# The second inverse stage's result written by DMA into the groups' y tiles, without the DRAM buffer between

## The chip, the core and the metric

The kernel runs on one core of a Trainium2 chip. The core has TensorE for matmuls (PE in the profile, with its weight loads as PEld), VectorE (DVE), ScalarE (ACT) and GpSimd (POOL) for elementwise work, SyncE (SP), which here issues the DMAs, and 16 DMA engines that move data between DRAM (HBM) and on-chip memory (SBUF). Matmul results land in PSUM. Each engine runs its own instructions in order and waits for others by semaphores. The metric is the device time of one execution in microseconds, smaller being better.

## The reference

Two stages follow one another over an input of 8 batches, 3136 tokens and 256 channels: a filter in the frequency domain along the tokens, and a block of Fourier mixing, normalization and a two-layer MLP.

```python
X = np.fft.rfft(x, axis=1)
y = np.fft.irfft(X * (filt_r + 1j * filt_i), n=3136, axis=1)
mixed = np.real(np.fft.fft(np.fft.fft(y, axis=1), axis=2))
u = y + mixed
un = (u - mean(u)) / np.sqrt(var(u) + 1e-06)      # over the channels
out = u + np.maximum(un @ w_ch1, 0) @ w_ch2       # 256 -> 1024 -> 256
```

The filtered spectrum is used twice: transformed back it gives y, and, since the transform of y along the tokens is that spectrum again, a second transform over the channels gives `mixed`.

## The kernel before

The transform of length 3136 = 112 x 28 is made by matmuls in two stages each way. Forward stage one (`forward1`, tiles x and s1) works on 14 pieces of a batch and stores them to a DRAM buffer d1 (L357); stage two reads them back transposed in order (at, L378), multiplies (s2), applies the filter, transposes the result by DMA (z, L427) and keeps the folded spectrum in SBUF for the channel mix (eo). Inverse stage one (`inverse1`, i1, L463 to L465) multiplies z and stores bt to a DRAM buffer d2 (L469). Inverse stage two (`inverse2`) loads d2 in seven chunks of a batch (tile b2, printed as b, L501, two buffers), multiplies (y in PSUM, L520), copies the result to the staging tile ys on ScalarE (L528, three buffers) and stores it to the DRAM buffer dy (L505): four DMAs a chunk, six for the first.

Tokens are kept as 1568 slots of a batch; a slot holds the pair of tokens of a frequency and its negative (kind 0 and 1). The MLP goes over all 8 x 1568 slots in 49 groups of 256 slots, two tiles of 128 slots each. `fetch(g)` loads a group's y from dy (L575) into a tile y of 128 x 2 x 2 x 256 floats, of which there are four. `prepare(g)` makes the channel mix (L588), adds it to y (L598), normalizes (L655 to L678), splits into high and low halves (u16, L683) and transposes by DMA (ut, L684). `first_product` (h, L706) and `second_product` (acc, L735) are the MLP in eight steps of 128 hidden channels; behind the eighth the result is added to y (L744) and stored (out, L747).

One loop over the 49 x 8 steps sets the order: in each step a first product, a second product two steps behind, then `advance` (forward stages and inverse stage one of the next batch) and `give` (steps of inverse stage two: one that loads, two that wait, seven chunks), each up to a number that follows the step. `bring` sees to it that a group's chunks are issued before it is fetched. `after(...)` puts an instruction behind a marked one on its own engine; the first fetch sets the mark ("y", 0), behind which the x loads of batch 1 are issued (L326):

```python
with after(("y", 0), ("un", 0)) if b == 1 else nullcontext():
    if q < 7:
        nc.sync.dma_start(xs[q], a["x"][b, :, 4 * q : 4 * q + 4])
```

Behind that, a scheduler orders each engine's instructions by its own estimate of times. The raw weights, loaded in the first part, share the buffers of ys and ut (`LOAD_IN`).

Of the kernel before, what the change touches and what calls it, by code (L numbers as in the profile page):

```python
# [9 lines left out]
F32 = mybir.dt.float32  # L10
# [18 lines left out]
EXPO = 0x7F800000  # L29
LAG = 2  # L30
AHEAD = 4

# [10 lines left out]
LOADED = 300  # L43
LOAD_AT = (15, 16, 17, 18, 19, 29, 30, 27)
LOAD_AFTER = (6, 7, 8, 9, 10, None, None, None)
LOAD_IN = ("ys", "ys", "ys", "ut", "ut", "ys", "ys", "ys")
WIDEN_AT = (22, 22, 30, 54, 55, 56, 57, 57)
BOUND_AT = (65, 72)
SPLIT_AT = (65, 101)
# [10 lines left out]
def slot_freqs():  # L60
    k = np.zeros((56, 28), np.int64)
    k2 = np.arange(28)
    for U in range(56):
        j, s = divmod(U, 2)
        if U == 0:
            k[0] = np.where(k2 < 14, 112 * k2, 56 + 112 * (k2 - 14))
        else:
            k1 = 28 if U == 1 else (j if s == 0 else 56 - j)
            k[U] = k1 + 112 * k2
    return k  # L70

# [18 lines left out]
def constants():  # L90
# [5 lines left out]
    for U in range(56):  # L96
        j, s = divmod(U, 2)
        th2 = 2 * np.pi * ((n2[:, None] * k[U][None]) % N) / N
        if U == 0:
            s1[:, 0, 0] = 1  # L100
            s1[:, 0, 1] = np.where(n1 % 2, -1, 1)
            lo = n2 < 14
            s2[0, 0, :, 0, :] = np.cos(th2) * lo
            s2[0, 0, :, 1, :] = -np.sin(th2) * lo
            s2[0, 1, :, 0, :] = np.cos(th2) * ~lo
            s2[0, 1, :, 1, :] = -np.sin(th2) * ~lo
            s2[0, 0, :, 1, 0] = np.where(n2 % 2, -1, 1)
        else:
            k1 = 28 if U == 1 else (j if s == 0 else 56 - j)
            th = 2 * np.pi * ((n1 * k1) % 112) / 112  # L110
            s1[:, U, 0] = np.cos(th)
            s1[:, U, 1] = -np.sin(th)
            s2[U, 0, :, 0] = np.cos(th2)
            s2[U, 1, :, 0] = np.sin(th2)
            s2[U, 0, :, 1] = -np.sin(th2)
            s2[U, 1, :, 1] = np.cos(th2)
# [38 lines left out]
    for jp in range(2):  # L155
        for kind in range(2):
            for s in range(2):
                h = s if kind == 0 or jp == 0 else 1 - s
                for q in range(28):
                    n = tok[kind, 2 * jp + s, q]  # L160
                    assert residue(h, jp) == n % 56
                    th = 2 * np.pi * ((n // 56 * j) % 56) / 56
                    a, b = 2 * np.cos(th), -2 * np.sin(th)
                    a[0] = 1
                    b[0] = (-1) ** (n // 56)
                    i2[jp, h, 0, :, 28 * kind + q] = a * 2048 / N
                    i2[jp, h, 1, :, 28 * kind + q] = b * 2048 / N

    s2h, s2l = split16(s2)
    s2h, s2l = s2h.reshape(56, 56, 56), s2l.reshape(56, 56, 56)  # L170
# [22 lines left out]
def _program(ctx, tc, nc, a, NB):  # L193
# [75 lines left out]
    for t in y16s:  # L269
        nc.gpsimd.memset(t[:, :, :, 112:], 0.0)  # L270

    sxs, alphas, dys, esps = {}, {}, {}, {}

    mF = tp.tile([128, 12], F32, tag="mF", name="mF", bufs=1)

# [212 lines left out]
            load(c + far)  # L488

    def inverse2(b, d2):  # L490
        dy = dp.tile([2, NS, 256], F32, tag="dy", name=f"dy_{b}", bufs=3)
        dys[b] = dy
        d2v = d2.rearrange("(m r) j l c -> (r j l) m c", r=2)
        al = alphas[b]
        bts = {}

        def load(c):
            if c < 7:
                bts[c] = fp.tile([112, 4, 2, 256], F16, tag="b2", name=f"b2_{b}_{c}", bufs=2)
                with after("dy"):  # L500
                    nc.sync.dma_start(bts[c].rearrange("p j h c -> p (j h) c"), d2v[:, 8 * c : 8 * c + 8])  # L501

        def store(k, s, r, ys, c, j0):
            rows = dy[k, 224 * c : 224 * c + 224].rearrange("(j s q) c -> s q j c", j=4, s=2)
            marks["dy"] = nc.sync.dma_start(rows[s, :, j0], ys[r : r + 28, j0]).ins  # L505

        load(0)
        for _ in range(1 + WAIT):
            yield
        for c in range(7):  # L510
            load(c + 1)
            bt = bts.pop(c)
            ys = fp.tile([128, 4, 256], F32, tag="ys", name=f"ys_{b}_{c}", bufs=3)
            ps = [bank(f"y_{b}_{c}_{o}").rearrange("p (j c) -> p j c", j=2) for o in range(2)]
            with after("pe") if c == 0 else nullcontext():
                for o, p in enumerate(ps):
                    for js, t in [(slice(0, 1), 0), (slice(1, 2), 1)] if c == o == 0 else [(slice(0, 2), 1)]:
                        for i in range(2):
                            for h in range(2):
                                nc.tensor.matmul(  # L520
                                    p[64 * h : 64 * h + 64, js],
                                    i2[:, t, h, i],
                                    bt[:, 2 * o + js.start : 2 * o + js.stop, h],
                                    start=i == 0,
                                    stop=i == 1,
                                )
            for o, p in enumerate(ps):
                nc.scalar.activation(ys[:, 2 * o : 2 * o + 2], p, AF.Copy, scale=al[:, 2:3])  # L528
            for s in range(2):
                store(0, s, 64 * s, ys, c, slice(0, 4))  # L530
                if c:
                    store(1, s, 64 * (1 - s) + 28, ys, c, slice(0, 4))
                else:
                    store(1, s, 64 * s + 28, ys, c, slice(0, 1))
                    store(1, s, 64 * (1 - s) + 28, ys, c, slice(1, 4))
            yield

    d2s = {}
# [25 lines left out]

    ys_of = {}

    def fetch(g):
        y = ys_of[g] = mp.tile([128, 2, 2, 256], F32, tag="y", name=f"y_{g}", bufs=4)
        for t, (g0, g1) in enumerate(groups[g]):
            q = g0  # L570
            while q < g1:
                b = q // NS
                e = min(g1, (b + 1) * NS)
                with after(("ut", 0)) if g == 2 else after(("out", g - 4)):
                    marks["y", g] = nc.sync.dma_start(  # L575
                        y[q - g0 : e - g0, t], dys[b][:, q - b * NS : e - b * NS].rearrange("k s c -> s k c")
                    ).ins
                q = e

    def channels(p, lhs, start, stop):  # L580

# [187 lines left out]
    def load_weights(i):  # L769
        name = ("w1", "w2")[i // 4]  # L770
        src = a[name][:, i % 4 // 2, 512 * (i % 2) : 512 * (i % 2) + 512]
        if a[name].dtype == F32:
            words[i] = src
            return
        pool, bufs = {"ut": (mp, 2), "ys": (fp, 3)}[LOAD_IN[i]]
        words[i] = pool.tile([128, 512, 2], I32, tag=LOAD_IN[i], name=f"raw_{i}", bufs=bufs)
        with after(("d1", LOAD_AFTER[i])):
            nc.sync.dma_start(words[i], src.bitcast(I32).rearrange("p (n w) -> p n w", w=2))

    def widen_weights(i):  # L780
        name = ("w1", "w2")[i // 4]
        if i % 4 == 0:
            raws[name] = [], tp.tile([128, 5], F32, tag="mw", name="m" + name)
        ws, m = raws[name]
        if name == "w1":
            w = mp.tile([128, 512], F32, tag="h", name=f"w_{i}", bufs=4)
        else:
            if i % 2 == 0:
                pairs[0] = mp.tile([128, 2, 512], F32, tag="y", name=f"w_{i}", bufs=4)
            w = pairs[0][:, i % 2]  # L790
        ws.append(w)
        if a[name].dtype == F32:
            nc.sync.dma_start(w, words[i])
        else:
            with after("ylo" if "ylo" in marks else ("dve", 13)):
                widen(w, words[i], f"{i}")
        squares(m[:, i % 4 : i % 4 + 1], w, f"{i}")
# [32 lines left out]

    nc.sync.dma_start(s1, a["c_s1"])
    forth, home = steps(there), steps(back)
    done, come = [0], [0]

    def advance(n):

# [7 lines left out]
    def give(n):  # L844

        while come[0] < min(n, NB * BACK) and done[0] >= STEPS * (come[0] // BACK + 1) - 1:
            next(home)
            come[0] += 1

# [45 lines left out]
    while come[0] < need(255):  # L895
        weigh(STEPS + come[0])
        give(come[0] + 1)
    fetch(0)
# [6 lines left out]
    fetch(1)  # L905
    work = prepare(1)
    for _ in range(AHEAD):
        next(work, None)
# [1 line left out]
    for q in range(8 * ng + LAG):  # L910
        g, f = divmod(q, 8)
        if g < ng:
            first_product(g, f)
        if f == 8 - AHEAD:
            for _ in work:
                pass
            if g + 2 < ng:
                work = prepare(g + 2)
        next(work, None)
        if q >= LAG:  # L920
            second_product(*divmod(q - LAG, 8))
        advance(int(STEPS * (1 + min((q + 1) / RISE, (q + 1) / per + EARLY))))
        give(min(come[0] + 1, soon(32 * q + SOON)))
        if f == 0 and g + 2 < ng:
            bring(groups[g + 2][-1][1] - 1)
            fetch(g + 2)


def device_arrays(x, filt_r, filt_i, moe_w_ch1, moe_w_ch2):
# [51 lines left out]
```

## Time and profile before

| | us |
|---|---|
| median of 3 runs | 1581.63 |
| lowest and highest of them | 1572.67, 1591.9 |
| profiled execution, span from first to last instruction | 1585.0 |
| busy PE, DVE, ACT, POOL in it | 1407.5, 1092.9, 771.9, 541.5 |

The profile gives no time of that execution beside its span. It was taken in one execution; the span in 40 equal slices of 39.6 us, each digit the busy share or the granted clock in tenths, shows the two parts:

```profile
PE   4443899888989889899989999899999999999998
DVE  7774787677767776687756876687766876554552
PEclk9555899989999989999999999999999999999999
DMA  7989468879985787748983689748983799544321
```

In the first four slices the first batch goes through its stages, TensorE is less than half busy and its granted clock is about half; behind them the MLP runs and TensorE is busy nearly throughout, while the DMA engines have a cycle of some 180 us, one batch. A row of the waits names the engine and line that waited, what released it, the total, the number and the longest; a row of the timeline gives start and duration, and in brackets the idle time before it.

### The profile page before, as it was taken

What the parts mean: (1) busy time and instruction counts of PE and PEld (TensorE: products, weight loads), DVE (VectorE), ACT (ScalarE), POOL (GpSimd) and SP (SyncE); (2) the same over time, 40 slices, a digit from 0 to 9 for tenths busy, and PEclk for the clock granted to TensorE, in tenths of its full rate; (3) what the DMA queues carried; (4) which work ended last, traced back from release to release, by engine and by line L of the source; (5) the groups of instructions that cost most, each with busy time, mean ns of one, the idle gap of its engine ahead of it and who ended that gap; (6) DMA issues with size and microseconds to landing.
All of it is one profiled execution on the core that took longest, in us unless ns stands there. A gap on an engine that the chain in (4) does not pass through costs nothing.

```text
span 1585.0 us, 30178 instructions
## 1 busy us (share of the span) xinstructions
PE 1407.5 (89%) x11217; PEld 940.7 (59%) x11217; DVE 1092.9 (69%) x2409; ACT 771.9 (49%) x1442; POOL 541.5 (34%) x675
## 2 busy tenths in 40 slices
PE   4443899888989889899989999899999999999998
PEld 1331566545766557566766666665765667666666
DVE  7774787677767776687756876687766876554552
ACT  4455364365536445365544545365554655434432
POOL 4462019405711266004821076003830086001100
PEclk9555899989999989999999999999999999999999
DMA  7989468879985787748983689748983799544321
GB/s 226 257 204 240 109 157 182 199 196 197 200 224 129 179 172 177 193 128 203 220 221 86 192 194 194 208 126 196 210 228 97 196 216 182 133 110 124 78 67 41
DMA packets 446260, 273.13 MB, mean 172 GB/s; under 512 B 235392, under 2 KB 412592, under 8 KB 446112
## 3 DMA queue, kind: packets, MB, share of 16 engines
q1 hardware_dynamic: 446112, 271.20, 71.3%
q8 instruction: 88, 1.44, 0.4%
q14 instruction: 60, 0.49, 0.1%
HBM read 113.31 MB, written 102.76 MB: 136 GB/s over the span
## 4 chain that ended last, share of the span: by engine, by line
PE 63%; DMA 17%; DVE 10%; POOL 3%; issue 3%; ACT 3%; SPq 1%; DVEq 0%; ACTq 0%; POOLq 0%
PE h L706 25%; PE acc L735 23%; PE s L353 4%; DMA b<-d 4%; PE y L520 3%; DMA z<-y 3%; DMA d<-bt 3%; DMA ut<-u 2%; DMA at<-d 2%; PE mix L588 2%; DVE y L598 2%; DVE mx L262 2%; DVE h L716 1%; DMA d<-ast 1%; PE i L463 1%
## 5 line engine op out<-in xcount | busy, mean ns | idle before, releaser
L706 PE MATMUL h<-ut,w1s 128*128 128x512 f16 x2352 | 598.4, 389 | 20.1 <-DMA ut<-u 17.1
L735 PE MATMUL acc<-w2s,h 128*128 128x256 f16 x4704 | 599.0, 274 | 1.9 <-DVE y L744 1.9
L735 PEld LDWEIGHTS <-h 128*128 128x128 f16 x4704 | 456.9, 98 | 143.0 <-issue 17.0
L716 DVE SCALAR_TENSOR_TENSOR h<-h,h 128x512 f16<-128x512 f32 x392 | 268.1, 685 | 304.7 <-ACT h L715 303.8
L715 ACT ACTIVATE h<-h 128x512 f16<-128x512 f32 x392 | 233.2, 595 | 450.2 <-PE h L706 443.8
L706 PEld LDWEIGHTS <-w1s 128*128 128x128 f16 x2352 | 227.2, 99 | 240.2 <-issue 43.7
L683 POOL TENSOR_TENSOR u<-un,u 128x512 f16<-128x512 f32 x94 | 108.4, 1167 | 729.6 <-ACT u L681 633.7
L598 DVE SCALAR_TENSOR_TENSOR y<-mix,alpha,y 128x508 f32<-128x508 f32 (+1 forms) x368 | 156.2, 475 | 16.8 <-PE mix L588 14.7
L520 PE MATMUL y<-b,i 112*64 112x512 f16 (+1 forms) x480 | 76.5, 424 | 55.8 <-DMA b<-d 49.2
L422 POOL TENSOR_TENSOR y<-yt,y 128x448 f16<-128x448 f32 x105 | 110.9, 1058 | 33.8 <-ACT y L418 33.3
L678 ACT ACTIVATE un<-y,sb 128x256 f32<-128x256 f32 x196 | 101.7, 590 | 32.4 <-DVE sb L671 30.4
L353 PE MATMUL s<-x,s 112*112 112x512 f16 x336 | 106.8, 415 | 9.6 <-DVE x L348 5.0
L468 DVE TENSOR_TENSOR bt<-i,bt 112x512 f16<-112x512 f32 x112 | 75.8, 682 | 53.7 <-ACT bt L467 53.2
L528 ACT ACTIVATE ys<-y,alpha 128x512 f32<-128x512 f32 x112 | 75.3, 685 | 74.2 <-PE y L520 74.0
L414 POOL TENSOR_TENSOR yt<-yt,t 128x224 f32<-128x224 f32 x105 | 69.1, 658 | 116.4 <-DVE t L410 62.3
L467 ACT CAST bt<-i 112x512 f16<-112x512 f32 x112 | 65.1, 582 | 80.5 <-PE i L465 70.5
L356 DVE TENSOR_TENSOR ast<-s,ast 112x512 f16<-112x512 f32 x112 | 76.6, 684 | 29.0 <-ACT ast L355 25.9
L348 DVE SCALAR_TENSOR_TENSOR x<-x,sx,x 112x512 f16<-112x512 f32 x111 | 87.9, 802 | 6.0 <-ACT x L347 5.8
L401 PE MATMUL s<-s,at 112*128 112x56 f16 x896 | 64.0, 192 | 30.9 <-DMA at<-d 22.4
L347 ACT ACTIVATE x<-x,sx 112x512 f16<-112x512 f32 x111 | 78.9, 724 | 22.3 <-DVE sx L259 20.8
L463 PE MATMUL i<-z,i 112*112 112x256 f16 x224 | 65.7, 293 | 26.4 <-DMA z<-y 19.6
L418 ACT CAST y<-yt 128x448 f16<-128x448 f32 x112 | 62.5, 563 | 51.6 <-POOL yt L415 46.7
(129 smaller groups left out, 1611.7 us busy)
## 6 DMA issues: line engine op xcount, KB each, us to landing
x<-x SPq DMA_DIRECT2D x56, 448.0 KB
d<-ast SPq DMA_DIRECT2D x112, 224.0 KB
at<-d SPq DMA_DIRECT2D x56, 448.0 KB
d<-bt SPq DMA_DIRECT2D x112, 224.0 KB
b<-d SPq DMA_DIRECT2D x56, 448.0 KB
out<-y SPq DMA_DIRECT2D x98, 256.0 KB
y<-dy SPq DMA_DIRECT2D x92, 256.0 KB
dy<-ys SPq DMA_DIRECT2D x208, 112.0 KB
```

Source lines behind the costliest of these rows:

```text
L348: nc.vector.scalar_tensor_tensor(x16[:, 1], x, sx[:112, 1:2], x16[:, 0], op0=ALU.mult, op1=ALU.subtract)
L353: marks["pe", q] = nc.tensor.matmul(p, s1[:, hs], x16[:, hx], start=i == 0, stop=i == 2).ins
L422: last = half(b, hf == 1).tensor_tensor(y16[:, :, 1, :112], ytv, y16[:, :, 0, :112], op=ALU.subtract)
L463: nc.tensor.matmul(p[:, i], i1[:, j + i, 0], z[:, i, 0], start=True, stop=False)
L520: nc.tensor.matmul(p[64 * h : 64 * h + 64, js], i2[:, t, h, i], bt[:, 2 * o + js.start : 2 * o + js.stop, h], start=i == 0, stop=i == 1,)
L598: nc.vector.scalar_tensor_tensor(out, p, al, y, op0=ALU.mult, op1=ALU.add)
L678: nc.scalar.activation(un[:m, k], y[:m, t, k], AF.Identity, bias=sb[:m, i, 1:2], scale=sb[:m, i, 3:4])
L683: marks["u16", g] = low.tensor_tensor(u16[:m, :, :, 1], unv, u16[:m, :, :, 0], op=ALU.subtract).ins
L706: marks["pe"] = nc.tensor.matmul(p[:, c0 : c0 + n].rearrange("p (t k q) -> p t k q", k=2, q=m), w1s[:, d, hw, 128 * f : 128 * f + 128], ut ...
L715: nc.scalar.activation(h[:, 0, :nt], p[:, :nt], AF.Relu)
L716: marks["h"] = nc.vector.scalar_tensor_tensor(h[:, 1, :nt], p[:, :nt], 0.0, h[:, 0, :nt], op0=ALU.max, op1=ALU.subtract).ins
L735: nc.tensor.matmul(acc[:m, k], h[:, hh, c0 : c0 + m], w2s[:, f, hw], start=f == 0 and k == 0 and i == 0, stop=f == 7 and k == 1 and i == 2,)
```

## The change

- `dy`, `store` and `fetch` go. `place` writes rows of ys by DMA straight into the y tiles of the groups. One DMA carries 56 slots (or 28, in the first rows of a batch) of one j and one kind, and is split where a tile of 128 slots ends.
- The two residues of a pair are now j and j + 28 for both kinds (k1 = j + 56 s in place of j and 56 - j), and the columns of the i2 constants are set so that a half of ys (64 rows) holds 56 slots of one kind.
- A y tile is taken when its first slot is written (`y_tile`). There are five of them, and two of ys instead of three. The raw weights that lay in ys lie in y tiles.
- `give` does not issue a chunk, nor the three steps ahead of chunk 0, while the chunk's last slot lies in a group that needs more than five tiles beyond the groups finished (`gone`).
- The marks ("y", g), and with them the order of the loads of x of batch 1, have gone with `fetch`.

```diff
-LOAD_IN = ("ys", "ys", "ys", "ut", "ut", "ys", "ys", "ys")
+LOAD_IN = ("y", "y", "y", "ut", "ut", "y", "y", "y")
...
-            k1 = 28 if U == 1 else (j if s == 0 else 56 - j)
+            k1 = 28 if U == 1 else j + 56 * s
...
-                h = s if kind == 0 or jp == 0 else 1 - s
+                h = kind if jp else s
+                col = 28 * (s if jp else kind)
...
-        dy = dp.tile([2, NS, 256], F32, tag="dy", name=f"dy_{b}", bufs=3)
...
-        def store(k, s, r, ys, c, j0):
-            rows = dy[k, 224 * c : 224 * c + 224].rearrange("(j s q) c -> s q j c", j=4, s=2)
-            marks["dy"] = nc.sync.dma_start(rows[s, :, j0], ys[r : r + 28, j0]).ins
+        def place(ys, r, n, j, kind, slot):
+            while n:
+                tile_, p = divmod(slot, 128)
+                m = min(n, 128 - p)
+                y = y_tile(tile_ // 2)
+                marks["dy"] = nc.sync.dma_start(y[p : p + m, tile_ % 2, kind], ys[r : r + m, j]).ins
+                r, n, slot = r + m, n - m, slot + m
...
-            ys = fp.tile([128, 4, 256], F32, tag="ys", name=f"ys_{b}_{c}", bufs=3)
+            ys = fp.tile([128, 4, 256], F32, tag="ys", name=f"ys_{b}_{c}", bufs=2)
...
-            for s in range(2):
-                store(0, s, 64 * s, ys, c, slice(0, 4))
-                if c:
-                    store(1, s, 64 * (1 - s) + 28, ys, c, slice(0, 4))
-                else:
-                    store(1, s, 64 * s + 28, ys, c, slice(0, 1))
-                    store(1, s, 64 * (1 - s) + 28, ys, c, slice(1, 4))
+            for j in range(4):
+                slot = b * NS + 224 * c + 56 * j
+                for h in range(2):
+                    if c or j:
+                        place(ys, 64 * h, 56, j, h, slot)
+                    else:
+                        for kind in range(2):
+                            place(ys, 64 * h + 28 * kind, 28, j, kind, slot + 28 * h)
...
-    def fetch(g):
-        y = ys_of[g] = mp.tile([128, 2, 2, 256], F32, tag="y", name=f"y_{g}", bufs=4)
...
-                with after(("ut", 0)) if g == 2 else after(("out", g - 4)):
-                    marks["y", g] = nc.sync.dma_start(
...
+    def y_tile(g):
+        if g not in ys_of:
+            ys_of[g] = mp.tile([128, 2, 2, 256], F32, tag="y", name=f"y_{g}", bufs=YBUFS)
+        return ys_of[g]
...
+            b, c = divmod(come[0], BACK)
+            c -= 1 + WAIT
+            if (b * NS + 224 * max(c, 0) + 223) // 256 >= gone[0] + YBUFS:
+                return
             next(home)
             come[0] += 1
...
             second_product(*divmod(q - LAG, 8))
+            gone[0] = (q - LAG + 1) // 8
```

The scheduler then gives another order. At the end of inverse stage one of batch 4, on ScalarE, before (h16 is the relu behind eight such h of a group, sb, un and u16 belong to the normalization of group 22, ys_4_0 is the first copy out of the second inverse stage; the last copy of inverse stage one, bt_4_6_1, stands two rows above the first row):

```order
L715 ACTIVATE h16_21_0_10043<-h_21_0_10036 128x512
L662 ACTIVATE sb_22_10022<-mv_22_10012,eps_88 128x4
L715 ACTIVATE h16_21_1_10073<-h_21_1_10066 128x512
L678 ACTIVATE un_22_0_10076<-y_22_9721,sb_22_10022 128x256 x2
L678 ACTIVATE un_22_1_10134<-y_22_9721,sb_22_10022 128x256 x2
L715 ACTIVATE h16_21_2_10131<-h_21_2_10124 128x512
L681 CAST u16_22_0_10079<-un_22_0_10076 128x4x128
L528 ACTIVATE ys_4_0_10101<-y_4_0_0_10102,alpha_4_8472 128x512
```

And now, with the same rows above the first:

```order
L714 ACTIVATE h16_21_0_10185<-h_21_0_10178 128x512
L457 CAST eo_89<-ef_4_6_10324 128x2x160
L661 ACTIVATE sb_22_10164<-mv_22_10154,eps_88 128x4
L714 ACTIVATE h16_21_1_10212<-h_21_1_10205 128x512
L677 ACTIVATE un_22_0_10215<-y_22_9114,sb_22_10164 128x256 x2
L677 ACTIVATE un_22_1_10250<-y_22_9114,sb_22_10164 128x256 x2
L680 CAST u16_22_0_10218<-un_22_0_10215 128x4x128
L714 ACTIVATE h16_21_2_10247<-h_21_2_10240 128x512
L680 CAST u16_22_1_10253<-un_22_1_10250 128x4x128
L714 ACTIVATE h16_21_3_10278<-h_21_3_10271 128x512
L714 ACTIVATE h16_21_4_10300<-h_21_4_10293 128x512
L533 ACTIVATE ys_4_0_10354<-y_4_0_0_10355,alpha_4_8594 128x512
```

The copy to ys, and on TensorE the y matmuls that it reads, stand behind h_21_3 and h_21_4 now, two steps of the MLP later.

On SP, where batch 5 goes from forward stage one (stores of ast to d1) to stage two (loads of at), before (ys_4_3 is a chunk of batch 4):

```order
L357 DMA d1_5_10216<-ast_5_12_10808 112x1024
L357 DMA d1_5_10216<-ast_5_13_10855 112x1024
L505 DMA dy_4_9998<-ys_4_3_10955 28x4x256
L684 DMA_TRANSPOSE ut_24_10738<-u16_24_0_10828 128x8x128
L684 DMA_TRANSPOSE ut_24_10738<-u16_24_1_10872 128x8x128
L378 DMA at_5_0_10894<-d1_5_10216 112x8x256
```

And now, with the last d1 store, ast_5_13, three rows above the first row:

```order
L509 DMA y_26_10621<-ys_4_2_10993 48x256
L509 DMA y_26_10621<-ys_4_2_10993 8x256
L509 DMA y_26_10621<-ys_4_2_10993 48x256
L509 DMA y_26_10621<-ys_4_2_10993 56x256
L683 DMA_TRANSPOSE ut_24_10873<-u16_24_0_10960 128x8x128
L509 DMA y_26_10621<-ys_4_2_10993 56x256
L509 DMA y_26_10621<-ys_4_2_10993 24x256
L509 DMA y_27_11015<-ys_4_2_10993 32x256
L509 DMA y_26_10621<-ys_4_2_10993 24x256
L509 DMA y_27_11015<-ys_4_2_10993 32x256
L683 DMA_TRANSPOSE ut_24_10873<-u16_24_1_11032 128x8x128
L380 DMA at_5_0_11054<-d1_5_10332 112x8x256
```

The chunk's placements and the transposes of group 24 stand between that store and the load.

On SP again, in the first part, where the y tiles of groups 0 and 1 are loaded and the x loads of batch 1 (x_1) follow, before (the last stores of inverse stage one, bt_0_6, and the first loads b2_0 stand some ten rows above):

```order
L575 DMA y_0_1151<-dy_0_1077 128x2x256
L501 DMA b2_0_3_1172<-d2_0_115 112x8x256
L575 DMA y_0_1151<-dy_0_1077 128x2x256
L575 DMA y_1_1346<-dy_0_1077 128x2x256
L326 DMA x_1_0_1404<-x 112x1024
L326 DMA x_1_1_1405<-x 112x1024
L505 DMA dy_0_1077<-ys_0_2_1174 28x4x256 x4
L501 DMA b2_0_4_1199<-d2_0_115 112x8x256
L326 DMA x_1_2_1406<-x 112x1024
L326 DMA x_1_3_1407<-x 112x1024
```

And now, with x_1_0 to x_1_3 directly above the first row:

```order
L328 DMA x_1_4_1404<-x 112x1024
L328 DMA x_1_5_1405<-x 112x1024
L328 DMA x_1_6_1406<-x 112x1024
L471 DMA d2_0_115<-bt_0_6_0_1056 112x1024
L471 DMA d2_0_115<-bt_0_6_1_1067 112x1024
L501 DMA b2_0_0_1077<-d2_0_115 112x8x256
L501 DMA b2_0_1_1079<-d2_0_115 112x8x256
L509 DMA y_0_1098<-ys_0_0_1081 28x256 x4
L509 DMA y_0_1098<-ys_0_0_1081 56x256 x2
```

The x loads of batch 1 have moved ahead of the last stores of inverse stage one and of the first loads of stage two.

More of the change, by code (lines that the diff above doesn't have):

```diff
@@ L31 @@
 AHEAD = 4
+YBUFS = 5
 PAUSE = 4
@@ L108, in constants @@
         else:
-            k1 = 28 if U == 1 else (j if s == 0 else 56 - j)
+            k1 = 28 if U == 1 else j + 56 * s
             th = 2 * np.pi * ((n1 * k1) % 112) / 112
@@ L165, in constants @@
                     b[0] = (-1) ** (n // 56)
-                    i2[jp, h, 0, :, 28 * kind + q] = a * 2048 / N
-                    i2[jp, h, 1, :, 28 * kind + q] = b * 2048 / N
+                    i2[jp, h, 0, :, col + q] = a * 2048 / N
+                    i2[jp, h, 1, :, col + q] = b * 2048 / N
     s2h, s2l = split16(s2)
@@ L270, in _program @@
         nc.gpsimd.memset(t[:, :, :, 112:], 0.0)
-    sxs, alphas, dys, esps = {}, {}, {}, {}
+    sxs, alphas, esps = {}, {}, {}
     mF = tp.tile([128, 12], F32, tag="mF", name="mF", bufs=1)
@@ L490, in inverse2 @@
     def inverse2(b, d2):
-        dy = dp.tile([2, NS, 256], F32, tag="dy", name=f"dy_{b}", bufs=3)
-        dys[b] = dy
         d2v = d2.rearrange("(m r) j l c -> (r j l) m c", r=2)
@@ L565, in _program @@
     ys_of = {}
-    def fetch(g):
-        y = ys_of[g] = mp.tile([128, 2, 2, 256], F32, tag="y", name=f"y_{g}", bufs=4)
[L569 to L573, printed above, removed]
-                with after(("ut", 0)) if g == 2 else after(("out", g - 4)):
[L575 to L578, printed above, removed]
+    def y_tile(g):
+        if g not in ys_of:
+            ys_of[g] = mp.tile([128, 2, 2, 256], F32, tag="y", name=f"y_{g}", bufs=YBUFS)
+        return ys_of[g]
     def channels(p, lhs, start, stop):
@@ L774, in load_weights @@
             return
-        pool, bufs = {"ut": (mp, 2), "ys": (fp, 3)}[LOAD_IN[i]]
+        pool, bufs = {"ut": (mp, 2), "y": (mp, YBUFS)}[LOAD_IN[i]]
         words[i] = pool.tile([128, 512, 2], I32, tag=LOAD_IN[i], name=f"raw_{i}", bufs=bufs)
@@ L788, in widen_weights @@
             if i % 2 == 0:
-                pairs[0] = mp.tile([128, 2, 512], F32, tag="y", name=f"w_{i}", bufs=4)
+                pairs[0] = mp.tile([128, 2, 512], F32, tag="y", name=f"w_{i}", bufs=YBUFS)
             w = pairs[0][:, i % 2]
@@ L832, in _program @@
     forth, home = steps(there), steps(back)
-    done, come = [0], [0]
+    done, come, gone = [0], [0], [0]
     def advance(n):
@@ L897, in _program @@
         give(come[0] + 1)
-    fetch(0)
     for i, _ in enumerate(prepare(0)):
@@ L904, in _program @@
     bring(511)
-    fetch(1)
     work = prepare(1)
@@ L925, in _program @@
             bring(groups[g + 2][-1][1] - 1)
-            fetch(g + 2)
 def device_arrays(x, filt_r, filt_i, moe_w_ch1, moe_w_ch2):
```

## The prediction

> **What bounds the kernel now.** I read the page first (engines, chain), then TensorE's own waits, then the places of the longest ones, then SP's queue. The page says who is full and who carries the end:
>
> ```profile
> PE 1407.5 (89%) x11217; PEld 940.7 (59%) x11217; DVE 1092.9 (69%) x2409; ACT 771.9 (49%) x1442; POOL 541.5 (34%) x675
> PE 63%; DMA 17%; DVE 10%; POOL 3%; issue 3%; ACT 3%; SPq 1%; DVEq 0%; ACTq 0%; POOLq 0%
> ```
>
> TensorE bounds the steady part, and DMA waits are the next share of the chain. TensorE's waits from 165 us to the end (us in total, times, longest):
>
> ```profile
> PE y L520 <- DMA b<-d: 28.4, 7, 6.5
> PE h L706 <- DMA ut<-u: 17.1, 7, 5.8
> PE s L401 <- DMA at<-d: 12.6, 12, 2.2
> ```
>
> The largest is the one beside the change: seven times, once for each batch from 1 to 7, TensorE stands before the first matmul of the second inverse stage (y, L520) until its input b has come back from DRAM. These are the seven places in TensorE's timeline:
>
> ```profile
> 316.00 1.06 PE L520 MATMUL y<-b,i 112*64 112x256 f16 x12 [3.27 <-DMA b<-d]
> ...
> 464.69 1.92 PE L520 MATMUL y<-b,i 112*64 112x256 f16 x12 [3.74 <-DMA b<-d]
> ...
> 653.98 1.92 PE L520 MATMUL y<-b,i 112*64 112x256 f16 x12 [5.54 <-DMA b<-d]
> ...
> 830.26 1.92 PE L520 MATMUL y<-b,i 112*64 112x256 f16 x12 [6.49 <-DMA b<-d]
> ...
> 1012.14 1.92 PE L520 MATMUL y<-b,i 112*64 112x256 f16 x12 [4.12 <-DMA b<-d]
> ...
> 1190.00 1.06 PE L520 MATMUL y<-b,i 112*64 112x256 f16 x12 [3.09 <-DMA b<-d]
> ...
> 1367.74 1.06 PE L520 MATMUL y<-b,i 112*64 112x256 f16 x12 [2.16 <-DMA b<-d]
> ```
>
> Around the longest, the chain (start, us, what) shows two transfers in series and then TensorE slow, beside its usual pace:
>
> ```profile
> 807.08 1.30 PE h L706 x6
> ...
> 808.77 1.31 PE acc L735 x12
> ...
> 817.01 8.28 DMA d<-bt
> 825.36 4.86 DMA b<-d
> 830.26 1.92 PE y L520 x12
> ...
> 833.90 2.56 PE h L706 x6
> ```
>
> Six h matmuls take 1.30 us before the wait and 2.56 us after it. The granted clock (the figure after POOL's busy time) in short windows behind six of the seven waits says why:
>
> ```profile
> 316.00:318.00 2.00, 2.00 (x17) 1.08 (x17) 0.25 (x3) 1.26 (x2) 0.00 (x0) 1.00 0.24 43
> 465.00:469.00 4.00, 4.00 (x24) 2.24 (x21) 0.00 (x0) 1.37 (x2) 0.00 (x0) 0.64 0.31 69
> 654.00:658.00 4.00, 4.00 (x18) 1.81 (x18) 0.00 (x0) 1.37 (x2) 0.00 (x0) 0.50 0.60 143
> 830.00:837.00 7.00, 6.74 (x33) 3.81 (x33) 0.00 (x0) 2.39 (x4) 1.15 (x1) 0.53 0.69 177
> 1012.00:1018.00 6.00, 5.86 (x32) 3.13 (x32) 0.00 (x0) 1.76 (x3) 0.00 (x0) 0.55 0.72 197
> 1190.00:1194.00 4.00, 4.00 (x27) 2.24 (x27) 0.07 (x1) 1.86 (x3) 0.00 (x0) 0.69 0.47 133
> ```
>
> At batches 2 to 6 the loss by the lower clock is 4 x 0.36 + 4 x 0.50 + 7 x 0.47 + 6 x 0.45 + 4 x 0.31 = 10.7 us on top of the wait itself; at batch 1 nothing.
>
> **The change: the wait for b.** The diff does not touch this load, but it adds a gate (a chunk is not started before one of five y tiles is free), and the order that is built from it puts more MLP matmuls between the last matmul of the first inverse stage and the first y. Counted on TensorE in the two orders, h and acc matmuls between them are, for batches 1 to 7, before: 12+34, 24+41, 24+48, 24+36, 24+44, 18+36, 24+41; now: 18+40, 90+179, 42+84, 36+72, 30+60, 24+48, 24+37. At 1.30/6 and 1.31/12 us each, with 0 to 24 small mix matmuls (estimated at 0.06 us, about half an acc matmul), the cover was 7.3, 10.2, 10.4, 9.1, 10.0, 7.8, 10.6 us and is 9.2, 40.7, 19.2, 16.6, 14.0, 11.3, 10.2 us. Old cover plus old wait is what the two transfers need: 10.6, 13.9, 15.9, 15.6, 14.1, 10.9, 12.8 us. Need less new cover leaves 1.4, 0, 0, 0, 0.1, 0, 2.6: about 4 us of the 28.4. So 24 us of waiting and the 10.7 us of slow clock go: -35 us. Against it: a wait that goes can return at the next one. The nearest rows are the 17.1 and 12.6 us above, nineteen waits, spread over the batches; if TensorE comes some 5 us earlier to one of them per batch, up to all 35 us returns. Ends: 0 and -35. I take -32, nearer the full end, because the at wait starts from a store of TensorE's own earlier result and moves with it, and the ut covers (below) mostly grow.
>
> **SP's queue.** All DMAs are issued by SP in order. Removed are 240 stores to dy and 104 loads of y from it; added are 631 placements (12 to 14 for the first chunk of a batch, 10 to 12 for each other, split where a tile ends). Their prices, and what the loads waited for (durations min/median/max in ns; then us in total, times, longest):
>
> ```profile
> L505 SPq DMA_DIRECT2D dy<-ys x240: 307/403/2717, 123.6 to 1480.5; - x120
> ...
> L575 SPq DMA_DIRECT2D y<-dy x104: 304/390/1746, 129.1 to 1504.9; - x104
> ```
>
> ```profile
> SPq L575 <- DMA out<-y: 72.5, 31, 5.2
> ...
> SPq L575 <- DMA dy<-ys: 24.7, 24, 2.7
> ```
>
> Issue: 631 x 0.40 = 252 us against 240 x 0.403 + 104 x 0.390 = 137 us, +115 us. The loads' waits, 97 us, go: the first placement into a tile now stands behind the output store of the group five before, mostly ten rows or more behind it, and the wait for dy does not exist. Net +18 us over 49 groups on a queue that is no bound by itself; bounds -97 and +115. But a burst of a dozen placements is 5 us in which a transpose or an at load stands behind them. One place shows it: for batch 5, eleven placements and two transposes stand between the last d1 store and the first at load (before: one store and two transposes), 10 x 0.4 = 4 us more, and the cover there grows by only 1.6 us. I take +8 us for TensorE: 2.4 at this place, and 0.13 at each of the 42 other chunks after the head. Ends 0 and +42 (a whole microsecond at each).
>
> Here a rule of the Trainium skill speaks against the change: "DMA: Bandwidth & Descriptors", section Bandwidth, calls transfers under 64 KB dominated by descriptors, and the placements are 56 KB and less where the stores were 112 KB. By its fit of 2.0 us plus bytes over 436 GB/s a placement of 56 KB is an estimated 2.1 us, and a chunk's twelve, if they went one behind the other, an estimated 25 us; the sum would then come out on the side of the second rival. Row L505 shows a queue that goes on after 0.40 us, so the sum stays with the row, and whether the landings pile up no row of this trace can say.
>
> **DMA traffic.** 25.7 MB written and 25.7 MB read become 25.7 MB from SBUF to SBUF.
>
> ```profile
> q1 hardware_dynamic: 446112, 271.20, 71.3%
> ```
>
> A packet takes 0.713 x 16 x 1585 us / 446112 = 40 ns on average; 25,088 packets of 1 KB fewer are 25,088 x 40 ns / 16 = 63 us of 1130 us. That is off the path except where the DMAs are full: ends 0 and -4 (6% of the 58 us of waits above), I take -2.
>
> **The head, to the first h.** The x loads of batch 1 were ordered behind the first y load; that mark is gone, and they now stand ahead of the last two stores of the first inverse stage (third place shown with the change). The chain, the DMA share (the figure before GB/s) and the rows around the first h:
>
> ```profile
> 4.08 11.79 DMA x<-x
> ...
> 115.02 2.24 DMA d<-bt
> 117.28 4.05 DMA b<-d
> ...
> 136.62 9.68 DMA b<-d
> 146.31 7.95 DMA y<-dy
> ```
>
> ```profile
> 105.00:110.00 5.00, 1.74 (x9) 1.32 (x7) 3.74 (x8) 2.69 (x5) 1.70 (x3) 0.50 0.62 121
> 110.00:115.00 5.00, 3.15 (x13) 2.47 (x13) 4.62 (x9) 2.62 (x7) 1.34 (x1) 0.50 0.39 117
> ```
>
> ```profile
> 156.01 5.18 SPq L684 DMA_TRANSPOSE ut<-u  x2
> ```
>
> ```profile
> 164.87 4.06 PE L706 MATMUL h<-ut,w1s 128*128 128x512 f16 x12
> ...
> 191.35 2.76 PE L706 MATMUL h<-ut,w1s 128*128 128x512 f16 x12 [1.40 <-DMA ut<-u]
> ```
>
> Seven x loads took 11.8 us at the start; put in at about 110 us they run to 121.5, so the stores land near 123 instead of 117.3: +6 us. Behind that the long 9.68 and 7.95 us, stretched by these same x loads, shrink to about the 4.05 us of an undisturbed b load, and the y loads are gone. But SP now issues 56 placements before ut instead of 22 stores and 4 loads (+30 x 0.4 = 12 us), and ScalarE writes chunk 3 only behind the normalization of group 0. I put ut at about 161 (156.01 before) and h at 167: +2 us. Chunks 5 and 6 of batch 0 move behind it: 16 matmuls at half of the 1.92 us for 8 that the head pays, +2 us. Group 1 is ready earlier: -1.4 us. Together +3; ends -6 (only the y loads' 7.95 us go, less 2) and +10 (the 6 us and 4 of SP's 12 come through).
>
> **The covers of ut.** Counted the same way, TensorE's work between a group's last mix and its first h falls by 2.4, 6.0, 2.3, 1.8 and 4.0 us at groups 3, 4, 8, 12 and 37 and grows by 6 to 10 us at groups 5, 11, 17, 23 and 29. Group 4 waits already:
>
> ```profile
> 291.68 5.30 PE L706 MATMUL h<-ut,w1s 128*128 128x512 f16 x12 [1.65 <-DMA ut<-u]
> ```
>
> There 6.0 us come in full, at group 12 perhaps 1: +7 less the b wait of batch 1 that goes: I take +5; ends -5 and +14.
>
> **At nothing.** The new pairing of residues changes constants alone: matmuls, ScalarE's copies and POOL's work stay the same in number, and POOL issues no DMA. The raw weights now lie in y tiles, and the first placement needs one that VectorE's widening has read; that is done while b is loaded, and if it were not, SP would stand there.
>
> **Sum.** -32 + 8 - 2 + 3 + 5 = -18, against the profiled span of 1585.0 us (the profile gives no time beyond it): 1567. That span is 3.4 us above the median of the three runs, 1581.63; from the median it is 1563.6, and I say 1563 us.
>
> **Rivals.**
> - *The wait moves (within 1%).* For it: chain work beside the b wait (8.28 us for d<-bt) is DMA, and waits for ut and at of 29.7 us follow. Against: the covers there. If half of the 35 us returns: -18 + 14.5 = -3.5, 1578 us. The y loads' trip through DRAM was hidden in the steady part anyway: it is no wait of TensorE's above.
> - *SP becomes the bound (slower).* The placements' landing times hold SP back: 12 in a row, and ut and z transposes behind them. It decides from 18/42 = 0.43 us lost on TensorE at each of 42 chunks beyond the +8. At a whole 1.0 us each and the b gain halved: -16 + 42 - 2 + 3 + 5 = +32, 1614 us. For it: bursts of 12 against 4. Against: the 97 us of waits that SP loses. The page of the Trainium skill named above is on this side.
> - *The y tile is free too late (slower).* A placement waits for the output store five groups back and blocks SP as the loads did, 72.5 us in all now. That is paid today with four tiles, so it costs more only where placements that stand on SP keep ScalarE from its two ys tiles, and TensorE from its banks: at the longest wait, 5.2 us, once a batch, 7 x 5.2 - 18 = +18, 1600 us. Against: in the new order the store stands ten rows or more ahead at most tiles.
>
> **Chances.** Forecast (faster, 1540 to 1566) 0.52, the wait moves 0.28, SP 0.12, the tile 0.08. Within 1%, 15.8 us, is about what a measurement of this kernel cannot tell from no change. So faster 0.52, same 0.30, slower 0.18. The range runs from -41 (all of -35, the head's -6, the rest 0) to +12, short of the two slower cases: 1540 to 1594. The forecast's own is 1540 to 1566.
>
> **What would show it.** Right: the y waits on b below 6 us in all, the clock at 1.00 behind most of them, SP's waits for out smaller than 72 us, first h between 162 and 172 us. Wrong: TensorE's waits for ut or at above 45 us together; ScalarE's ys or SP's placements waiting for DMA in tens of microseconds; the first h after 175 us.

## The result, and the profile after

| | before | changed |
|---|---|---|
| median, us | 1583.04 (1572.67 to 1591.9, 4 runs) | 1651.84 (1642.66 to 1655.15, 4 runs) |
| ratio, 95% interval | | 1.0427 (1.0382 to 1.0473) |

The changed kernel is slower by 4.3%; the prediction was 1563 us. The page of the changed kernel: its span and its chain by engine and by line (the kernel before had PE 63% and SPq 1%), and its DMA queue:

```profile
span 1647.5 us, 30693 instructions
PE 1418.1 (86%) x11217; PEld 946.4 (57%) x11217; DVE 1091.0 (66%) x2409; ACT 772.2 (47%) x1442; POOL 542.6 (33%) x675
PEclk9555799789999999999999999998999999999999
q1 hardware_dynamic: 424464, 245.52, 62.1%
PE 46%; DMA 18%; POOL 9%; issue 9%; DVE 9%; SPq 5%; ACT 3%; DVEq 0%; ACTq 0%; POOLq 0%
```

The engines' work is the same (TensorE's 1418.1 us against 1407.5 go with its lower clock, 0.926 against 0.939 in the mean), and the DMA engines do less; TensorE's share of the chain fell, and time in which SP issues DMAs entered it. TensorE's longest waits from 165 us on (total, times, longest):

```profile
PE h L705 <- DMA ut<-u: 54.3, 16, 13.4
PE i L465 <- DMA z<-y: 20.4, 8, 4.6
PE y L525 <- DMA b<-d: 16.0, 7, 3.9
PE s L403 <- DMA at<-d: 13.8, 11, 3.1
```

The wait for b went from 28.4 to 16.0 us, but ut from 17.1 to 54.3, and z from the 5.5 us of this row of the kernel before to 20.4. Of the 54.3 us, 13.4 are the wait for the first h itself, which in the kernel before came at 164.87 us without a wait for ut; behind the first h it is 40.9 us against 17.1. The row of z before:

```profile
PE i L463 <- DMA z<-y: 5.5, 6, 1.8
```

Both are transposes that SP issues behind placements. The placement's own row (durations in ns, minimum, median, maximum) tells why:

```profile
L509 SPq DMA_DIRECT2D y<-ys x632: 532/746/2996, 130.5 to 1554.3; - x158
```

A placement holds SP for 746 ns at the median, not for the 403 ns of a store to dy. SP's timeline in the head (start, us, what) has them back to back, five chunks ahead of the first ut, and TensorE's first h behind that:

```profile
130.48 9.38 SPq L509 DMA_DIRECT2D y<-ys  x12
139.96 0.47 SPq L501 DMA_DIRECT2D b<-d  x1
140.54 8.63 SPq L509 DMA_DIRECT2D y<-ys  x12
...
175.59 2.65 SPq L683 DMA_TRANSPOSE ut<-u  x2
```

```profile
180.23 4.22 PE L705 MATMUL h<-ut,w1s 128*128 128x512 f16 x12 [13.35 <-DMA ut<-u]
```

The first h was at 164.87 us: 15.4 us of the span's 62.5 are lost here. The other 47.1 us are lost behind it: from the first h to the end TensorE is idle 31.0 us longer (112.8 against 81.8) and busy 16.2 us longer with much the same matmuls (1354.5 against 1338.3, at a granted clock of 0.96 against 0.97). One such place is the longest later wait, of 7.21 us. There GpSimd has written the second half of u (two instructions, the last over at 807.21), and SP comes to the second transpose 11 us later, with nine placements of 6.3 us among the rows between. The rows are GpSimd's, SP's and TensorE's:

```profile
804.94 2.27 POOL L682 TENSOR_TENSOR u<-un,u 128x512 f16<-128x512 f32 x2 [2.47 <-ACT u L680]
```

```profile
809.37 1.26 SPq L429 DMA_TRANSPOSE z<-y  x1
810.68 2.73 SPq L509 DMA_DIRECT2D y<-ys  x4
813.52 1.26 SPq L683 DMA_TRANSPOSE ut<-u  x1
814.83 3.55 SPq L509 DMA_DIRECT2D y<-ys  x5
818.50 1.25 SPq L683 DMA_TRANSPOSE ut<-u  x1
```

```profile
821.62 2.74 PE L705 MATMUL h<-ut,w1s 128*128 128x512 f16 x6 [7.21 <-DMA ut<-u]
```

### The profile page after: what moved, and what is told of

The parts are those of the page before. It is cut to its first block, busy times and chain, and to the rows that moved or that the text cites. A ratio compares the mean times of both kernels' runs of the same rounds, so it can differ in the third digit from the quotient of the medians.

```text
span 1647.5 us, 30693 instructions
## 1 busy us (share of the span) xinstructions
PE 1418.1 (86%) x11217; PEld 946.4 (57%) x11217; DVE 1091.0 (66%) x2409; ACT 772.2 (47%) x1442; POOL 542.6 (33%) x675
## 3 DMA queue, kind: packets, MB, share of 16 engines
q1 hardware_dynamic: 424464, 245.52, 62.1%
## 4 chain that ended last, share of the span: by engine, by line
PE 46%; DMA 18%; POOL 9%; issue 9%; DVE 9%; SPq 5%; ACT 3%; DVEq 0%; ACTq 0%; POOLq 0%
PE h L705 18%; PE acc L734 17%; DMA d<-bt 4%; SPq L509 4%; PE s L355 3%; DMA ut<-u 3%; DMA z<-y 3%; PE y L525 2%; DMA at<-d 2%; DVE y L597 2%; POOL y L424 2%; DMA b<-d 2%; DMA d<-ast 2%; POOL yt L417 2%; DMA x<-x 2%
## 5 line engine op out<-in xcount | busy, mean ns | idle before, releaser
L705 PE MATMUL h<-ut,w1s 128*128 128x512 f16 x2352 | 603.5, 392 | 59.5 <-DMA ut<-u 54.3
L355 PE MATMUL s<-x,s 112*112 112x512 f16 x336 | 102.3, 407 | 9.4 <-DVE x L350 5.8
L416 POOL TENSOR_TENSOR yt<-yt,t 128x224 f32<-128x224 f32 x105 | 69.1, 658 | 112.8 <-DVE t L412 52.5
L408 DVE TENSOR_TENSOR yt<-s,ft 128x448 f32<-128x448 f32 x112 | 68.3, 615 | 36.5 <-PE s L404 31.2
```

The source lines that it names most:

```text
L355: marks["pe", q] = nc.tensor.matmul(p, s1[:, hs], x16[:, hx], start=i == 0, stop=i == 2).ins
L705: marks["pe"] = nc.tensor.matmul(p[:, c0 : c0 + n].rearrange("p (t k q) -> p t k q", k=2, q=m), w1s[:, d, hw, 128 * f : 128 * f + 128], ut ...
```

## The experiments

The theory to test: the issue of a placement costs SP 0.75 us, and what stands behind a burst comes late (issue theory). Its rivals: the transfers from SBUF to SBUF are slow or crowd the DMA engines, whoever issues them (landing theory); the gate, five y tiles and two ys tiles gave a worse order (order theory); the x loads of batch 1, put ahead, are the loss. All ratios are against the kernel before, run on the same chip. Each kernel is scheduled anew from its source, so neighbours of an edit move too; single waits are compared with that in mind.

**The price by itself (`price`).** Rows of twelve DMAs (K is 12), one shape after the other, on a chip that does nothing else. The part that issues them within SBUF:

```diff
+    def rows(n, w=256, p=0, r=0):
+        def issue(q, dst, src):
+            for i in range(K):
+                q.dma_start(dst[p : p + n, i, :w], src[r : r + n, i, :w])
+        return issue
```

> No part of the computation: rows of twelve DMAs back to back, one shape after the other, first all issued by SP, then all by ScalarE, with nothing else under way. Issue theory: from SBUF to SBUF, 56 rows of 1 KB hold SP for 0.70 to 0.80 us, 16 and 32 rows for 0.55 to 0.60; 28 rows to DRAM 0.30 to 0.40. The price goes with the number of rows and the destination, not with the bytes of a row. Landing or contention theory: with nothing else under way each placement holds SP for 0.45 us or less, as a store to DRAM does, and the 0.75 us of the changed kernel comes from full queues.

Issue durations from SP, by time: SBUF to SBUF with rows of 1 KB, 16, 28, 32, 56 and 128 rows, and 56 rows of 512 bytes; then to DRAM with 28 and 112 rows; then 56 rows, SBUF to SBUF, issued by ScalarE:

```profile
L214 SPq DMA_DIRECT2D dst<-src x12: 560/587/588, 18.8 to 25.7; - x12
...
L214 SPq DMA_DIRECT2D dst<-src x12: 746/746/762, 41.8 to 50.5; - x12
...
L214 SPq DMA_DIRECT2D dst<-src x12: 555/589/594, 54.4 to 61.3; - x12
...
L214 SPq DMA_DIRECT2D dst<-src x12: 746/746/799, 88.4 to 97.1; - x12
...
L214 SPq DMA_DIRECT2D dst<-src x12: 508/599/601, 134.9 to 141.9; - x12
...
L214 SPq DMA_DIRECT2D dst<-src x12: 746/746/829, 145.8 to 154.7; - x12
...
L221 SPq DMA_DIRECT2D buf<-src x12: 369/383/384, 209.8 to 214.5; - x12
...
L221 SPq DMA_DIRECT2D buf<-src x12: 308/444/452, 248.4 to 253.6; - x12
...
L214 ACTq DMA_DIRECT2D dst<-src x12: 757/763/794, 371.9 to 380.8; - x12
```

746 ns for 56 rows without any other traffic: the price is the instruction's own, not contention. In the shapes tried it depends on the destination and on the number of rows; for 56 rows it is the same with rows of 1 KB and of 512 bytes.

**The order alone (`before_gate`).** The kernel before with the gate, five y tiles, two ys tiles and the raw weights in y tiles; results still go through dy.

```diff
+            if (b * NS + 224 * max(c, 0) + 223) // 256 >= gone[0] + YBUFS:
+                return
...
-            ys = fp.tile([128, 4, 256], F32, tag="ys", name=f"ys_{b}_{c}", bufs=3)
+            ys = fp.tile([128, 4, 256], F32, tag="ys", name=f"ys_{b}_{c}", bufs=2)
```

> The kernel before (results still through DRAM), with only the order part of the change: five y tiles, two ys tiles, the raw weights in y tiles, and the gate in give. Issue theory: SP issues what it did, 1570 to 1595 us, TensorE's waits for ut below 25 us. Order theory: the 47 us that the changed kernel loses behind the first h come from here, 1615 to 1640 us.

1575.06 us, ratio 0.9977 (0.9955 to 0.9998); first h at 161.62 us. The order costs nothing, so the order theory falls. The issue theory had its number for ut wrong too: the waits for ut are above its 25 us. TensorE's waits from 165 us on, all behind the first h:

```profile
PE h L707 <- DMA ut<-u: 31.0, 13, 5.3
PE s L402 <- DMA at<-d: 14.2, 9, 5.8
PE i L464 <- DMA z<-y: 11.3, 6, 3.9
PE y L521 <- DMA b<-d: 6.4, 3, 4.1
```

The wait for b does shrink from 28.4 to 6.4 us here, as predicted, but ut, at and z together take back 13.9, 1.6 and 5.8 us.

**More issues in the kernel before (`before_split`, `split_half`).** The stores to dy cut into four, with the same bytes: in the first all of them, in the second those of one kind.

```diff
-            marks["dy"] = nc.sync.dma_start(rows[s, :, j0], ys[r : r + 28, j0]).ins
+            for j in range(j0.start, j0.stop):
+                marks["dy"] = nc.sync.dma_start(rows[s, :, j], ys[r : r + 28, j]).ins
```

> The kernel before, but each store to DRAM is split into its four parts: 896 stores of 28 rows of 1 KB instead of 240 of 28 rows of 4 KB, the same bytes. At 0.43 us from one to the next SP gets some 280 us more to issue (the changed kernel has 632 x 0.75 - 137 = 337 us more than the kernel before). Issue theory: 1610 to 1640 us, first h at 172 us or later, TensorE's waits for ut above 40 us. Order or landing theory: 1575 to 1595 us.

> The kernel before, with the stores of one kind split into four as in the run with all of them split: 560 stores instead of 240, some 138 us more on SP (896 stores and some 280 us made +74 us). If every microsecond of SP costs alike: about +36 us, 1605 to 1625 us. If the first 100 us or so are free and the loss sets in behind them (half the placements on GpSimd left SP with about 100 us more than the kernel before, at no loss): (138 - 100) / (280 - 100) x 74 = about +16 us, 1588 to 1602 us. GpSimd has no part in it.

`before_split`: 1653.66 us, ratio 1.0466 (1.0421 to 1.0512), more than the issue theory's 1640. `split_half`: 1585.69 us, ratio 1.0040 (1.0019 to 1.0061), less than both of its ranges. Rows of the first: the stores, TensorE's first h, and its waits from 165 us on (11.6 us of ut and 5.9 of b lie at or ahead of the first h):

```profile
L506 SPq DMA_DIRECT2D dy<-ys x896: 306/383/2441, 123.4 to 1551.6; - x180
```

```profile
183.40 4.33 PE L707 MATMUL h<-ut,w1s 128*128 128x512 f16 x12 [11.64 <-DMA ut<-u]
```

```profile
PE h L707 <- DMA ut<-u: 41.4, 16, 11.6
PE y L521 <- DMA b<-d: 35.9, 8, 7.8
PE i L463 <- DMA z<-y: 25.6, 11, 8.7
```

The whole loss appears without one transfer from SBUF to SBUF and without the new order: the landing theory falls as the main cause. And it is not proportional: 320 added stores cost 6 us, 656 cost 74.

**The destination of the pieces (`to_dram`).** The changed kernel; pieces that don't end a tile go to DRAM, and other data fills the y tile, so y is not the reference's.

```diff
+                to = y[p : p + m, tile_ % 2, kind] if p + m == 128 else dy[p : p + m, tile_ % 2, kind]
+                marks["dy"] = nc.sync.dma_start(to, ys[r : r + m, j]).ins
```

> The changed kernel, with its 632 pieces, but those that do not reach the end of a tile of 128 slots go to a DRAM buffer, and a y tile is filled by one load of other data (so y is not the reference's). 436 issues fall from about 0.7 us to 0.43, 49 loads of 0.4 come in: some 100 us less on SP, and more DRAM traffic. Issue theory: the loss goes down by a third or so, 1620 to 1638 us, first h at 174 us or earlier. Order theory: 1643 us or more.

1612.18 us, ratio 1.0211 (1.0172 to 1.0251), first h at 172.87 us: half of the loss goes, more than expected, with the same number of pieces and more DRAM traffic.

**Another queue (`half_act`, `half_pool`, `quarter_pool`, `all_pool`).** The same placements, some or all issued by another engine. The edit of `half_pool`; `half_act` has nc.scalar in it, `quarter_pool` the condition j == 3, and `all_pool` nc.gpsimd for all:

```diff
-                marks["dy"] = nc.sync.dma_start(y[p : p + m, tile_ % 2, kind], ys[r : r + m, j]).ins
+                q = nc.gpsimd if r >= 64 else nc.sync
+                marks["dy"] = q.dma_start(y[p : p + m, tile_ % 2, kind], ys[r : r + m, j]).ins
```

> The changed kernel, but the 316 placements of the upper half of ys are issued by ScalarE instead of SP. Issue theory (a placement holds SP for about 0.75 us, and b loads and ut and z transposes stand behind a dozen of them): SP loses 316 x 0.75 = 237 us of issuing, TensorE's waits for ut fall from 54 us to 25 or less and for z from 20 us to 10 or less, first h from 180 us to 172 or earlier; the time is 1600 to 1630 us (ScalarE pays for the issues). Landing theory (transfers from SBUF to SBUF are slow or crowd the DMA engines, whoever issues them): the same waits, 1640 to 1660 us. Order theory (the gate, five y tiles and two ys tiles gave TensorE a worse order): 1640 to 1660 us.

> The changed kernel, but the 316 placements of the upper half of ys are issued by GpSimd, which is busy a third of the time, instead of by ScalarE as in the run before. Issue theory: first h at 164 to 168 us as with ScalarE, TensorE's waits for ut 15 us or less, and if GpSimd's issues keep its own work back less than ScalarE's did (28.7 us of TensorE's waits were for ScalarE's h there), 1600 to 1630 us. Order theory: 1640 us or more, since what is lost behind the first h has nothing to do with the queue.

> The changed kernel, with only the placements of the fourth j (about 158 of 632) issued by GpSimd. Issue theory, if each microsecond of SP costs alike: SP loses about 119 of the 237 us that it loses with half of them, so the time lies half way between the changed kernel and the run with half on GpSimd, 1605 to 1625 us. If the loss comes only from the head and a few long bursts: 1595 us or less. If GpSimd's gain had another reason than SP's time: 1640 us or more.

> The changed kernel, with all 632 placements issued by GpSimd. SP then has 137 us less to issue than in the kernel before. If SP's time alone sets the result: 1565 to 1578 us, first h at 160 us or earlier. If GpSimd, which stood 262 us waiting for ys with half of them, becomes what is late (its lower parts of u and eo stand behind placements): 1585 to 1620 us, with TensorE's waits for ut or acc growing by 15 us or more.

With half on GpSimd the whole loss is gone: 1579.37 us, ratio 0.9990 (0.9966 to 1.0014), first h at 159.98 us. That is faster than the issue theory's 1600 to 1630 us, though the wait for ut stays above its 15 us. With a quarter, 1619.44 us, 1.0248 (1.0214 to 1.0282), in the range for a like price of each microsecond. The rows of `half_pool`, placements by queue and TensorE's wait for ut:

```profile
L510 POOL DMA_DIRECT2D y<-ys x318: 502/522/693, 131.1 to 1477.1; - x159
L510 SPq DMA_DIRECT2D y<-ys x314: 538/754/2804, 130.8 to 1479.3; - x157
```

```profile
PE h L706 <- DMA ut<-u: 19.7, 12, 6.5
```

With half on ScalarE the waits on SP's work shrink (ut behind the first h from 40.9 to 7.9 us, first h at 164.19 us, z from 20.4 to 13.6, not to the expected 10), yet the time stays at 1647.91 us, ratio 1.0432 (1.0396 to 1.0467): there ScalarE, whose relu TensorE needs for every h, is held by its own placements. From 668.21 to 675.11 us, for example, it issues eight in a row, its next relu comes only behind them, after 5.89 us without other work, and TensorE waits 3.49 us for it. TensorE's largest wait, and ScalarE's own waits:

```profile
PE acc L735 <- ACT h L715: 28.7, 17, 4.6
```

```profile
ACT h L715 <- PE h L706: 381.8, 212, 9.2
ACT h L715 <- DMA y<-ys: 49.4, 11, 6.8
```

With all on GpSimd, 1644.72 us, ratio 1.0400 (1.0356 to 1.0444), above both ranges, although first h comes at 157.36 us: the loss is behind it. GpSimd is busy for 866.8 us there, and SP waits 115.6 us for the u that GpSimd writes (77.7 in the changed kernel). How the loss divides among TensorE's waits is not settled in these two. That SP's queue was the cause and not only a place where the loss showed rests on `half_pool` beside `before_split`.

**What else stood in the head (`x_back`, `b_free`).** In the first, x of batch 1 is ordered behind y tile 0 again; in the second, b is not ordered behind the placements.

```diff
+                marks["y", tile_ // 2] = marks["dy"]
```

```diff
-                with after("dy"):
-                    nc.sync.dma_start(bts[c].rearrange("p j h c -> p (j h) c"), d2v[:, 8 * c : 8 * c + 8])
+                nc.sync.dma_start(bts[c].rearrange("p j h c -> p (j h) c"), d2v[:, 8 * c : 8 * c + 8])
```

> The changed kernel, but the x loads of batch 1 are ordered behind the last placement into y tile 0, as they were behind its load before. Issue theory: the head gains about the 7 us by which the first b load came later (124.7 us against 117.3), the rest stays: 1640 to 1650 us, first h at 172 to 176 us. Theory that the moved x loads are the main loss: 1620 us or less, first h at 168 us or earlier.

> The changed kernel, but the load of b is not ordered behind the placements of the chunk before the last. Issue theory: b leaves SP ahead of a dozen placements, so y's waits for b (16 us from 165 us on) fall to 8 us or less, but SP has as much to issue ahead of ut: first h stays within 5 us of 180, the waits for ut stay above 40 us, time 1630 to 1650 us. Theory that b alone is what comes late: first h at 170 us or earlier and 1620 us or less.

`x_back`: 1639.85 us, ratio 1.0379 (1.0335 to 1.0423), first h at 171.53 us, 8.7 earlier; its span, 1639.1 us, is 8.4 shorter than the changed kernel's, so the gain is in the head and the rest of the loss stays. `b_free`: 1644.62 us, ratio 1.0407 (1.0368 to 1.0446), no difference that the intervals show; TensorE waited 26.7 us for b, not 8 or less, and 64.1 us for ut, with first h at 181.17 us: a miss on b, and no sign that b's place behind the placements is what costs.

**Can both be beaten (`pool_x`, `pool_xb`, `gate_pool`)?** Half on GpSimd with the x mark back, then also with b free; and `before_gate` with its stores issued by GpSimd.

> Half of the placements on GpSimd, and the x loads of batch 1 ordered behind the first y tile as before. If the first b is late by the x loads alone: first h at 152 to 156 us instead of 160, and 1568 to 1576 us. If a y load's place in the order was there for nothing: 1577 to 1583 us.

> As the run with half of the placements on GpSimd and the x loads put back, and the load of b not ordered behind the placements. If b still stands behind bursts: TensorE's waits for b fall from 8 us to 4 us or less and the time is 2 to 6 us below that run's, 1564 to 1574 us. If not: within 3 us of it.

> The kernel before with the order part of the change, and its 240 stores to DRAM issued by GpSimd: SP has about 100 us less to issue than in the kernel before. If a microsecond of SP costs alike everywhere, down to there: 1555 to 1568 us. If there is a knee above the load of the kernel before, or GpSimd pays for it: 1570 to 1585 us.

1585.26, 1582.12 and 1586.41 us; ratios 1.0028 (1.0000 to 1.0056), 1.0007 (0.9984 to 1.0030) and 1.0046 (1.0020 to 1.0071). None gains, and the first and the last lie above all of their ranges; with the x loads put back the first h of `pool_x` comes at 161.11 us, no earlier than `half_pool`'s 159.98. In `gate_pool` a store costs GpSimd 583 ns, and TensorE waits 44.2 us for ut, 21.7 of them at the first h: less time on SP brings nothing further, and whether GpSimd's issuing pays for it was not separated. The only version whose interval lies below the kernel before is `before_gate`, by 0.2%.

**The runs against SP's time.** The sum of the durations of all DMA instructions of SP in each trace, with the number of them, for the kernels in which no other engine took more than half of the placements or stores and ScalarE none:

| kernel | SP's DMAs | us issuing | ratio |
|---|---|---|---|
| before | 1077 | 750 | 1 |
| before_gate | 1077 | 761 | 0.998 |
| pool_xb | 1047 | 809 | 1.001 |
| pool_x | 1047 | 816 | 1.003 |
| half_pool | 1047 | 817 | 0.999 |
| split_half | 1397 | 869 | 1.004 |
| quarter_pool | 1225 | 933 | 1.025 |
| to_dram | 1414 | 961 | 1.021 |
| before_split | 1733 | 1017 | 1.047 |
| changed | 1365 | 1052 | 1.043 |
| x_back | 1365 | 1055 | 1.038 |
| b_free | 1365 | 1039 | 1.041 |

Up to about 870 us of a span of 1585 the added time is nearly free; from there to the changed kernel 183 us more cost 3.9%, 61 us, a third of a microsecond each on average. The sum orders the kernels only roughly (`to_dram` loses less than `quarter_pool`), and it says nothing of the three left out, in which GpSimd issues all of them or ScalarE half: `gate_pool` 675 us and 1.005, `half_act` 806 and 1.043, `all_pool` 552 and 1.040. In the profiled executions the knee lies behind the first h: from there to the end it takes 1414 to 1422 us in the six kernels of up to 869 us, 1442 and 1438 at 933 and 961, and 1459 to 1468 above 1000. The head shows a cost earlier: the first h of `split_half` comes at 171.11 us, 6.2 later than before, and that is about all that it loses. SP is far from full over the span, but not in the bursts between which ut, z and b must leave; that the bursts make the knee is argued from the places shown, not tested by itself.

## Why the prediction was wrong

- **The step that failed** is the price in "SP's queue": "631 x 0.40 = 252 us against 240 x 0.403 + 104 x 0.390 = 137 us, +115 us". The row taken was that of stores to DRAM; the placements write to SBUF, at a median of 746 ns, 456 us for all 632 (631 were counted). SP's sum grew from 750 to 1052 us, +302. In the head, 56 placements took 42.2 us where 22.4 were counted. The marks named for a wrong forecast came with it: ut and at above 45 us together, and the first h after 175 us.
- **The loss on TensorE** was then taken as +8 and bounded at +42. With SP's time below the knee +8 was fair (`split_half`, +119 us on SP, lost 6 us); above it the bound was too small: the changed kernel lost 47.1 us behind the first h alone, with the gain at b already in it.
- **The rival "SP becomes the bound"** came true, with 0.12. Its mechanism was half right: ut and z did stand behind bursts on SP, but the landings were blamed, and `before_split` loses as much without a transfer between SBUF tiles, and `half_pool` loses nothing with all of them. The size rule of the Trainium skill ("DMA: Bandwidth & Descriptors", section Bandwidth) stood on the right side without being the mechanism. The fit used with it stands on that page of the Trainium skill in the section "Anatomy of one DMA — SWDGE (gpsimd) path", for DMAs that GpSimd issues, and it goes by bytes. From SP the issue time did not change from 56 KB to 28 KB, and GpSimd's 56 KB placements in `half_pool` landed 3.2 us after their issue at the median, above the estimated 2.1.
- **The wait for b (-32)**: the covers were read rightly. With the new order alone the wait went to 6.4 us, but the rival "the wait moves" took most of the gain, and `before_gate` is 4 us faster, not 32. The mistake is the end chosen between 0 and -35. In the changed kernel the wait stayed at 16.0 us, above the 6 named as the mark.
- **DMA traffic (-2)**: the queue's busy time fell by more than the 63 us worked out (71.3% of 1585.0 us to 62.1% of 1647.5, some 107 us), and no run shows a gain from it.
- **The head (+3)**: +15.4. x ahead of the last stores costs 8.7 us in the changed kernel, and the rest goes with SP's price; with half on GpSimd the head is 4.9 us shorter than before, x loads included, and putting x back gains nothing there.
- **The covers of ut (+5)**: `before_gate` has 13.9 us more wait for ut, in the range named (up to +14), but how much of it is cover and how much the b wait moved on can't be told apart.
- **At nothing, and the y tile too late**: that nothing would be lost there was right. SP's wait for out is 12.1 us in the changed kernel (72.5 before), and for ys 47.4 (74.8):

```profile
SPq L509 <- ACT ys L533: 47.4, 16, 9.2
...
SPq L509 <- DMA out<-y: 12.1, 9, 2.3
```

Had the price been 0.40 us as assumed, SP's sum would have been some 865 us, at the knee, and `half_pool` and `split_half` suggest what the change would then have given: no difference. So the price accounts for the loss, and the forecast gain of 18 us would have been missed all the same, for the end taken for the wait for b.

## What to carry to other kernels

Count a DMA's issue as work of the queue that issues it, and take its price from a row with the same destination and the same number of rows; if there is no such row, bound it well above the rows of another kind. Replacing a trip through DRAM by many small transfers between SBUF tiles loses if that queue has no time between the transfers that TensorE waits for, and here it gained nothing even where it had: look at the bursts and at what stands behind them, not at the queue's average. A second queue can take the issues, but its engine pays for each one in order: here GpSimd could take half of them and not all, ScalarE not even half.

## What the runs showed of the hardware

- From SP, an SBUF to SBUF DMA holds the queue for 746 ns with 28 or 56 rows of 1 KB (`price`; with 56, for rows of 512 and 256 bytes as well), for 714 and 707 with 24 and 40, and for 587 to 599 ns with 16, 32, 48, 64, 96, 112 or 128 rows: the 128-row one moves more than twice as much as the 56-row one in less issue time. To DRAM it is 383 ns with 28 rows and 444 ns with 112. ScalarE's queue has nearly the same price (763 ns for 56 rows), GpSimd's 522 ns at the median of the placements in `half_pool`.
- The Trainium skill, "DMA: Bandwidth & Descriptors", section "Why a DMA increments its semaphore by 16 and not by 1", says that a copy goes to the largest number of engines up to 16 that divides its rows, and that on SP and ScalarE the issuing sequencer itself writes the remaining increments. 24, 28, 40 and 56 rows are dearer than 16, 32 and 128, as that would have it; to DRAM, 28 rows are no dearer than 112, so the runs do not show it to be the reason.
- The same page of the Trainium skill, section "Issuing engines are not separate DMA queues", calls the time saved by issuing from several engines usually small relative to the DMA itself. Here it was not small: moving half of the placements to GpSimd took away the whole 4.3% (`half_pool`).
